# A routed-attention and expert kernel: the first tiles' token numbers move one turn later and into another bank

## The chip, the cores and the metric

The kernel runs on one core of a Trainium2 chip. A time is device microseconds (us) of one execution; before the change the median of three runs was 732.02 us (731.34 to 732.61). The profile is of one further execution, with a span of 725.9 us, and all times inside it count from its start.

The names of the engines: PE is TensorE (matrix products), PEld its weight loads, DVE is VectorE, ACT is ScalarE, POOL is GpSimd, SP is the engine that issues most transfers.

## The reference

Attention, in which a query sees only the keys of its own cluster, and then a layer of eight experts, of which each token goes to one:

```python
# q, k, v: (4, 8, 768, 64); centroids: (8, 16, 64); clusters by cosine similarity
mask = q_assign[:, :, :, None] == k_assign[:, :, None, :]
scores = np.where(mask, q @ k.T / 8, -1e9)                 # per batch and head
x = softmax(scores) @ v                                    # then (B*S, H*D) = (3072, 512)

logits = x @ w_gate                                        # (3072, 8)
expert_idx, gate_w = argmax(logits), softmax(logits)[expert_idx]
y = gate_w * (relu(x @ w1[expert_idx]) @ w2[expert_idx])   # w1: 512 -> 1024, w2: 1024 -> 512
```

## The kernel before

The attention goes through 16 pairs of heads (`g`, four pairs to each of four batches), two **turns** to a pair, so 32 turns. A turn has six scores (blocks of 128 keys against 384 queries for both heads), some jobs, six attends (values times the exponentials), and more jobs. A table, filled by `at(turn, part, function, ...)`, says which job is recorded where; the engines keep that order, each for itself:

```python
for n in range(-4, NTURN + 5):
    for x in range(n * NB, (n + 1) * NB):      # NB = 6
        if 0 <= x < NU:
            score(x)
        if x == n * NB + 2:
            for f, a in jobs.get((n, 2), ()): f(*a)      # part 2: between the scores
    for f, a in jobs.get((n, 0), ()): f(*a)              # part 0: before the attends
    for x in range(n * NB, (n + 1) * NB):
        if 0 <= x < NU:
            attend(x)
    for f, a in jobs.get((n, 1), ()): f(*a)              # part 1: after them
```

A score takes one of three double banks of PSUM, named `sps`; `wide()` hands out the same three to other work. The bank `mps` is a single one, for sums and small things. `T` gathers the exponentials' sums on VectorE:

```python
def score(u):
    ps = ps_s.tile([P, 2, 512], F32, name="sps")          # bufs=3
    # two products q.k (L991), two with the clusters' one-hots ohT (L994)
    nc.scalar.activation(A[u], ps[:, :, 0:HS], AF.Exp, scale=D**-0.5)     # L996
    # T <- A[u-1] + A[u] (L999), then T <- T + A[u] (L1003), on VectorE

def attend(u):      # twelve products O <- v, A in all for a turn (L1011)
def finish(g, half):                                       # after the attends of a half
    nc.scalar.copy(XT[g][...], O.pop((g, half))[...])      # L1019
def similar(g):     # clusters of the pair to come
    ps = wide()[:, 0, :]
    ...
    nc.vector.transpose(sims[g], ps[:, 0:HS])              # L911
def put_k(g):       # their one-hots go to ohT by four transfers on the SP queue (L961)
def weigh(g):       # denominators and gate logits of a pair
    ps = ps_m.tile([P, 512], F32, name="mps")
    ...             # 8 products with T, 4 with xT (L1033)
    nc.vector.transpose(ls, ps[:, 0:SQ])                   # L1041
    # reciprocal on VectorE; three or four small operations on GpSimd (the last pair: VectorE)
def keep(g, c0, c1):      # the pair's rows, undivided, to DRAM: a transpose (L1060), 4 transfers by GpSimd (L1062)
def keep_pads(b):         # the batch's factors for its rows: 16 transfers on the SP queue (L1097)
```

The experts' work begins inside the attention. When three of four batches are through the gate, the tokens of experts 0 and 1 among them fill the "first tiles" (288 and 128 tokens). Their numbers come out of one-hot products; `spread` turns them into row indices; GpSimd gathers the rows, 32 tokens to an issue; VectorE multiplies them by their factors and turns them; then the first layer's products can run:

```python
def tokens1():
    ps = wide()[:, 0, 0 : 2 * NP]
    tokens(ps, oh_r1, oh_c1, NF)                  # 18 products (L688)
    rc1[1] = indices(pl, ps, NP, s_idx1)          # seven small VectorE operations (L695 to L709)
def spread1():                                    # four products into mps (L716), five VectorE operations (to L723)
def gather1(i):                                   # 9 issues for i = 0, 4 for i = 1 (L289)
def turn_rows1(i):
    divide_rows(g)                                # VectorE, L302
    turn_rows(g)                                  # VectorE, L305
def first_half(i, f0=0, f1=FB):                   # layer 1 of first tile i (L318), relu on ScalarE (L328)

n = (NG - HP) * TG                                # turn 24
at(n + 4, 1, tokens1)
at(n + 5, 2, spread1)
for i in range(len(FT)):
    at(n + 5, 2, gather1, i)
at(n + 6, 1, turn_rows1, 0)
at(n + 7, 1, turn_rows1, 1)
```

After turn 31 come the first tile's products, the last pair's weighing, the gate of the last batch, and then the routing of all the rest (counts L642, token numbers, gathers) beside the second layer of the first tile (L383), and the remaining experts.

Of the kernel before, what the change touches and what calls it, by code (L numbers as in the profile page):

```python
# [8 lines left out]
F32 = mybir.dt.float32  # L9
# [11 lines left out]
NB = 6  # L21
XU = 8
RQ = 32
FT = ((128, 128, RQ), (128,))

NP = sum(len(n) for n in FT)
# [159 lines left out]
def kernel(  # L186
# [12 lines left out]
    B, H, S, D = q.shape  # L199
    C = centroids.shape[1]  # L200
    P = 128
# [3 lines left out]
    HP = H // 2  # L205
    NG = B * HP
# [27 lines left out]
    def fetch1(e, i):  # L234
        w1 = wpool.tile([P, DB, F], F32, name=f"w1_{i % 2}")
        nc.sync.dma_start(out=w1, in_=moe_w1[bass.ds(e, 1)].rearrange("e (a p) f -> p (e a) f", p=P))
        return w1

    def fetch2(e, i):
        w2 = wpool.tile([P, FB, Dm], F32, name=f"w2_{i % 2}")  # L240
        nc.sync.dma_start(out=w2, in_=moe_w2[bass.ds(e, 1)].rearrange("e (a p) d -> p (e a) d", p=P))
        return w2
# [25 lines left out]
    ps_m = late.enter_context(tc.tile_pool(name="ps_m", bufs=1, space=PSUM))  # L268
# [9 lines left out]
    def wide():  # L278
        return pools["s"].tile([P, 2, 512], F32, name="sps")
# [406 lines left out]
    def tokens(ps, oh_r, oh_c, n):  # L686
        for t in range(n):
            nc.tensor.matmul(  # L688
                ps, lhsT=oh_r[:, t, :], rhs=oh_c[:, t].rearrange("p i w -> p (i w)"), start=(t == 0), stop=(t == n - 1)
            )  # L690
# [11 lines left out]
    def indices(pool, ps, w, si):  # L702

        parts = pool.tile([P, 2 * w], BF16, name="hlb")
        nc.vector.tensor_copy(parts, ps)
        tv, ta = numbers(pool, ps[:, 0:w], ps[:, w : 2 * w], [P, w])
        nc.vector.tensor_scalar(tv, tv, scalar1=0.0, scalar2=float(2 * N), op0=ALU.is_lt, op1=ALU.mult)
        nc.vector.tensor_add(tv, tv, ta)
        nc.vector.tensor_copy(si, tv)  # L709
        return parts  # L710
# [21 lines left out]
    with ExitStack() as actx:  # L732
# [66 lines left out]
        ps = ps_m.tile([P, 512], F32, name="mps")  # L799
# [184 lines left out]
        def score(u):  # L984
            g, half, j = where(u)
            qs = slice(half * HS, (half + 1) * HS)
            ks = slice(j * P, (j + 1) * P)
            ps = ps_s.tile([P, 2, 512], F32, name="sps")
            for a in range(2):
                r = slice(a * D, (a + 1) * D)  # L990
                nc.tensor.matmul(ps[:, a, 0:HS], lhsT=qk[g][r, 1, ks], rhs=qk[g][r, 0, qs], start=True, stop=False)  # L991
            for a in range(2):
                r = slice(a * D, (a + 1) * D)
                nc.tensor.matmul(ps[:, a, 0:HS], lhsT=ohT[g][r, 1, ks], rhs=ohT[g][r, 0, qs], start=False, stop=True)  # L994
            A[u] = ap.tile([P, 2, HS], F32, name="A")
            nc.scalar.activation(A[u], ps[:, :, 0:HS], AF.Exp, scale=D**-0.5)  # L996
            if j == 1:
                T[g, half] = tp_.tile([P, 2, HS], F32, name="T", bufs=3)
                nc.vector.scalar_tensor_tensor(  # L999
                    T[g, half], in0=A[u - 1], scalar=1e-9 / P, in1=A[u], op0=ALU.add, op1=ALU.add  # L1000
                )
            elif j > 1:
                nc.vector.tensor_tensor(T[g, half], T[g, half], A[u], op=ALU.add)  # L1003

        def attend(u):
            g, half, j = where(u)
            if j == 0:
                O[g, half] = ps_o.tile([P, 512], F32, name="O")
            a_ = A.pop(u)
            for a in range(2):  # L1010
                nc.tensor.matmul(  # L1011
                    O[g, half][a * D : (a + 1) * D, 0:HS], lhsT=rows[g, "v"][:, a, j, :], rhs=a_[:, a, :],
                    start=(j == 0), stop=(j == NQ - 1),
                )
# [90 lines left out]
        def at(n, part, f, *a):  # L1105
            jobs.setdefault((n, part), []).append((f, a))
# [3 lines left out]
        TG = UG // NB  # L1110
# [4 lines left out]
        for g in range(NG):  # L1115
            n = g * TG
            if g == 0:
                at(-4, 0, turn, g, 0)
                at(-4, 0, load_next)
                at(-4, 0, blocks)  # L1120
                at(-4, 1, turn, g, 1)
                at(-3, 0, similar, g)
                at(-3, 0, assign, g)
                at(-3, 0, assign2, g)
                at(-3, 0, put, g)
            elif g == 1:
                at(-2, 1, idle_of, 20)
                at(0, 0, turn_blocks, g)
                for f in (similar, assign, assign2, put_k):
                    at(0, 1, f, g)  # L1130
                at(1, 0, put_q, g)
            else:
                at(n - 3, 0, turn_blocks, g)
                at(n - 2, 0, similar, g)
                at(n - 2, 0, assign, g)
                at(n - 2, 1, assign2, g)
                at(n - 2, 1, put_k, g)
                at(n - 1, 0, put_q, g)
            at(n, 1, finish, g, 0)
            at(n + 1, 1, finish, g, 1)  # L1140
            if g < NG - 1:
                at(n + 2, 0, weigh, g)
                at(n + 2, 1, keep, g, 0, S)
                if g % HP == HP - 1:
                    at(n + 3, 0, gate, g // HP)
                    at(n + 4, 0, gate2, g // HP)
                    at(n + 5, 0, keep_pads, g // HP)


        front = parts[0]  # L1150
# [13 lines left out]
            one_hots(pl, rc1[0], slice(i * NF // 2, (i + 1) * NF // 2), k_["tiles"], oh_r1, oh_c1)  # L1164

        def tokens1():
            ps = wide()[:, 0, 0 : 2 * NP]
            tokens(ps, oh_r1, oh_c1, NF)
            rc1[1] = indices(pl, ps, NP, s_idx1)

# [21 lines left out]
        n = (NG - HP) * TG  # L1192
# [2 lines left out]
        at(n + 2, 1, slots1)  # L1195
        at(n + 3, 0, one_hots1, 0)
        at(n + 3, 1, one_hots1, 1)
        at(n + 4, 1, tokens1)
        at(n + 5, 2, spread1)
        for i in range(len(FT)):  # L1200
            at(n + 5, 2, gather1, i)
        at(n + 6, 1, turn_rows1, 0)
        at(n + 7, 1, turn_rows1, 1)

        n = NG * TG
        at(n - 1, 0, keep, NG - 1, 0, HS)
        at(n, 0, keep, NG - 1, HS, S)
        at(n, 0, first_half, 0, 0, FB // 4)
        at(n, 0, weigh, NG - 1)
        at(n, 0, gate, B - 1)  # L1210
        at(n, 0, gate2, B - 1)
        at(n, 0, keep_pads, B - 1)
        at(n, 1, first_half, 0, FB // 4, FB // 2)
        at(n + 1, 0, first_half, 0, FB // 2, FB)
        for g in range(2, NG):
            at(max(g * TG - 6, -1), 1, load_qk, g)
            at(max(g * TG - 5, -1), 1, load_v, g)

        def early(e, i):

            if i == 0:
                weights[e] = (
                    wpool.tile([P, DB, F], F32, name=f"w1_{e}"), wpool.tile([P, FB, Dm], F32, name=f"w2_{e}"),
                )
            for w, src in zip(weights[e], (moe_w1, moe_w2)):
                n = w.shape[1] // DB
                nc.scalar.dma_start(
                    out=w[:, i * n : (i + 1) * n, :],
                    in_=src[e, i * n * P : (i + 1) * n * P, :].rearrange("(a p) f -> p a f", p=P),
                )  # L1230
# [5 lines left out]
        for n in range(-4, NTURN + 5):  # L1236
            for x in range(n * NB, (n + 1) * NB):
                if 0 <= x < NU:
                    score(x)
                if x == n * NB + 2:  # L1240
                    for f, a in jobs.get((n, 2), ()):
                        f(*a)
            for f, a in jobs.get((n, 0), ()):
                f(*a)
# [3 lines that stand above are left out]
            for f, a in jobs.get((n, 1), ()):  # L1248
                f(*a)
# [7 lines left out]
    with tc.tile_pool(name="sm", bufs=1) as sm:  # L1257
# [20 lines left out]
        for part in parts:  # L1278
            n, over = part["n"], part["over"]
# [97 lines left out]
    g = groups[0]  # L1377
# [58 lines left out]
    with tc.If(more > 0):  # L1436
        nx = nc.values_load(xe[0:1, NX : NX + 1], min_val=0, max_val=NX)
        general = nc.values_load(xe[0:1, NX + 1 : NX + 2], min_val=0, max_val=1)
        with tc.If(nx > XU):
            with ExitStack() as ectx:  # L1440
# [3 lines left out]
                with tc.For_i(XU, nx, 1) as i:  # L1444
# [5 lines left out]
                    g = dict(  # L1450
                        n=[P], rows=N, w=(fetch1(ex, 0), fetch2(ex, 0)), gi=lambda j, i: gi[:, i : i + 1],
                        si=lambda j: gi[:, 4:5], apart=False,
                    )
# [37 lines left out]
```

## Time and profile before

| engine | busy, us | share of the span |
|---|---|---|
| PE | 690.4 | 95% |
| PEld | 443.8 | 61% |
| DVE | 484.8 | 67% |
| ACT | 265.7 | 37% |
| POOL | 249.8 | 34% |

The table is the first part of the page. A share is an average over all stages; a change in one stage has to be read there. The other parts used below are the span in 40 slices (a digit is the busy share in tenths), the chain of work that ended last, followed back from the end, and the timeline: start and length in us, engine, line, operation, output and inputs, shapes and count, and in brackets how long the engine was idle before and what released it. "Remote" there means that no instruction or transfer in the trace ended when the awaited signal came.

Where the stages lie: turns 24 to 31 run from 268.95 to 353.5 us; turn 28's first score starts at 298.44, turn 29's at 309.81, turn 30's at 327.82, turn 31's at 338.00. The first tile's products run from 353.52 to 370.6, the second layer's from 370.82.

### The profile page before, as it was taken

To read this page: it belongs to the slowest core of one execution; us is meant where nothing else is said; L and a number is where in the kernel's file an instruction comes from. 1 tells how busy PE (TensorE), PEld (TensorE's weight loads), DVE (VectorE), ACT (ScalarE), POOL (GpSimd) and SP (SyncE) were. 2 spreads that over 40 slices of the span, in tenths; PEclk is the share of its full clock that TensorE was granted. 3 is DMA by queue.
4 is the path that set the end of the run, shared out by engine and by line. 5 is a ranking of instruction groups with operands and counts; after the bars stand their busy time and mean duration, and the time that the engine had idled before them with its cause. 6 is when DMAs were issued, how large, how long until landed. Compare 5 with 4: busy or idle time off the path is not lost.

```text
span 725.9 us, 12017 instructions
## 1 busy us (share of the span) xinstructions
PE 690.4 (95%) x4603; PEld 443.8 (61%) x4603; DVE 484.8 (67%) x769; ACT 265.7 (37%) x410; POOL 249.8 (34%) x327
## 2 busy tenths in 40 slices
PE   8999999999999999968999888999999999999994
PEld 6444444444444444433566647888878788987861
DVE  5898888878898789984555443967566756645300
ACT  4566556666556555633211012131211212121100
POOL 4022221222222221347305754445446363413101
PEclk9999999999999999989899999999999999999997
DMA  8345677787666644221234143778576667748530
GB/s 149 64 88 92 130 149 148 130 145 139 123 118 114 109 82 85 31 31 47 44 119 163 53 154 115 296 267 287 165 279 210 245 230 273 268 155 306 211 133 19
DMA packets 152420, 108.20 MB, mean 149 GB/s; under 512 B 116513, under 2 KB 122529, under 8 KB 152354
## 3 DMA queue, kind: packets, MB, share of 16 engines
q1 hardware_dynamic: 138146, 78.89, 40.0%
q0 software_dynamic: 8640, 19.63, 11.9%
q10 hardware_dynamic: 5568, 8.83, 4.1%
q8 instruction: 38, 0.62, 0.4%
q14 instruction: 28, 0.23, 0.1%
HBM read 93.06 MB, written 13.30 MB: 147 GB/s over the span
## 4 chain that ended last, share of the span: by engine, by line
PE 61%; issue 15%; POOL 6%; DVE 6%; SPq 4%; another core or an unknown queue 3%; DMA 3%; ACT 1%; ACTq 0%; POOLq 0%; DVEq 0%
PE sps L991 15%; PE O L1011 12%; PE sps L495 8%; PE sps L318 7%; PE sps L383 5%; PE sps L517 5%; PE sps L994 4%; POOL xg L289 3%; POOL out_dram L338 2%; SPq L1097 2%; PE mps L1033 2%; DMA ohT<-kv 1%; PE sps L354 1%; PE sps L904 1%
## 5 line engine op out<-in xcount | busy, mean ns | idle before, releaser
L991 PE MATMUL sps<-qk 64*128 64x384 f32 x768 | 163.8, 504 | 9.7 <-DVE tv L697 4.3
L289 POOL DMA_INDIRECT xg<-x_rows,g_idx x104 | 118.0, 1134 | 130.4 <-DVE xgT L305 80.2
L996 ACT ACTIVATE A<-sps 128x768 f32<-128x768 f32 x192 | 150.8, 813 | 30.8 <-PE sps L994 29.4
L1003 DVE TENSOR_TENSOR T<-T,A 128x768 f32<-128x768 f32 x128 | 122.7, 958 | 16.5 <-ACT A L996 3.0
L1011 PE MATMUL O<-A,v_in 128*64 128x384 f32 x768 | 131.0, 491 | 0.0
L991 PEld LDWEIGHTS sps<-qk 64*128 64x128 f32 x768 | 68.1, 191 | 64.2 <-issue 45.9
L1011 PEld LDWEIGHTS O<-A,v_in 128*64 128x64 f32 x768 | 52.4, 137 | 74.9 <-issue 72.2
L1045 POOL COPY dens<-ls 128x12 f32<-128x12 f32 x16 | 3.1, 195 | 208.6 <-DVE ls L1041 208.6
L994 PE MATMUL sps<-ohT 64*128 64x384 bf16 x384 | 65.6, 328 | 2.4 <-DMA ohT<-kv 2.4
L383 PE MATMUL sps<-w,h_sb 128*128 128x512 f32 x144 | 65.1, 606 | 2.9 <-DVE h_sb L326 2.9
L338 POOL DMA_INDIRECT out_dram<-zo,s_idx x32 | 37.7, 1177 | 71.6 <-ACT zo L334 28.6
L1019 ACT COPY xT<-O 128x384 f32<-128x384 f32 x32 | 15.3, 478 | 108.8 <-PE O L1011 86.7
L318 PEld LDWEIGHTS sps<-xgT,w 128*128 128x128 f32 x448 | 51.0, 192 | 3.7 <-issue 3.7
L1062 POOL DMA_DIRECT2D x_rows<-xb x68 | 48.4, 719 | 10.9 <-DVE xb L1060 8.3
L318 PE MATMUL sps<-xgT,w 128*128 128x128 f32 x448 | 51.3, 275 | 0.0
L999 DVE SCALAR_TENSOR_TENSOR T<-A 128x768 f32<-128x768 f32 x32 | 30.6, 957 | 29.4 <-ACT A L996 29.0
L383 PEld LDWEIGHTS sps<-w,h_sb 128*128 128x128 f32 x144 | 27.3, 194 | 34.9 <-issue 31.1
L495 PE MATMUL sps<-xs,w1s 128*128 128x144 f32 x288 | 39.7, 293 | 3.3 <-issue 3.1
L495 PEld LDWEIGHTS sps<-xs,w1s 128*128 128x128 f32 x288 | 37.1, 193 | 8.9 <-issue 4.7
L994 PEld LDWEIGHTS <-ohT 64*128 64x128 bf16 x384 | 20.5, 95 | 29.2 <-DMA ohT<-kv 4.4
L361 ACT COPY zc<-sps 32x512 f32<-32x512 f32 x24 | 13.9, 578 | 60.5 <-PE sps L354 49.3
L328 ACT ACTIVATE h_sb<-sps 128x512 f32<-128x512 f32 (+1 forms) x18 | 9.6, 578 | 69.5 <-PE sps L318 59.9
(260 smaller groups left out, 922.2 us busy)
## 6 DMA issues: line engine op xcount, KB each, us to landing
w<-in_moe_w_dram SPq DMA_DIRECT2D x28, 2048.0 KB, 9.3
w<-in_moe_w_dram ACTq DMA_DIRECT2D x16, 512.0 KB, 6.2
v_in<-in_v_dram SPq DMA_DIRECT2D x16, 384.0 KB, 4.4
q_in<-in_q_dram SPq DMA_DIRECT2D x60, 96.0 KB, 3.6
k_in<-in_k_dram SPq DMA_DIRECT2D x60, 96.0 KB, 6.3
x_rows<-xb POOLq DMA_DIRECT2D x60, 96.0 KB
xg<-x_rows,g_idx POOLq DMA_INDIRECT x104
ohT<-kv SPq DMA_DIRECT2D x60, 24.0 KB, 4.6
```

The costliest lines, as they stand in the source:

```text
L289: nc.gpsimd.indirect_dma_start(out=g["xg"][:, n, :], out_offset=None, in_=x_q[0 : 4 * g["rows"], :], in_offset=bass.IndirectOffsetOnAxis(a ...
L318: nc.tensor.matmul(o, lhsT=g["w"][0][:, c, fb * P : (fb + 1) * P], rhs=g["xT"][:, c, :cols], start=(c == 0), stop=(c == DB - 1),)
L338: ins = nc.gpsimd.indirect_dma_start(out=out[:, :], out_offset=bass.IndirectOffsetOnAxis(ap=g["si"](j)[0:m], axis=0), in_=zo[0:m], in_offs ...
L383: nc.tensor.matmul(zp, lhsT=g["h"][:, fb, j * P : (j + 1) * P], rhs=g["w"][1][:, fb, :], start=(fb == 0), stop=(fb == FB - 1),)
L495: nc.tensor.matmul(o, lhsT=a[:, c, f * P : (f + 1) * P], rhs=b[:, c, :], start=(c == 0), stop=(c == KH - 1),)
L517: nc.tensor.matmul(ps[:, 0, 0:DH], lhsT=a[:, f, :], rhs=b[:, f, :], start=(f == 0), stop=(f == FH - 1),)
L991: nc.tensor.matmul(ps[:, a, 0:HS], lhsT=qk[g][r, 1, ks], rhs=qk[g][r, 0, qs], start=True, stop=False)
L994: nc.tensor.matmul(ps[:, a, 0:HS], lhsT=ohT[g][r, 1, ks], rhs=ohT[g][r, 0, qs], start=False, stop=True)
L996: nc.scalar.activation(A[u], ps[:, :, 0:HS], AF.Exp, scale=D**-0.5)
L1003: nc.vector.tensor_tensor(T[g, half], T[g, half], A[u], op=ALU.add)
L1011: nc.tensor.matmul(O[g, half][a * D : (a + 1) * D, 0:HS], lhsT=rows[g, "v"][:, a, j, :], rhs=a_[:, a, :], start=(j == 0), stop=(j == NQ - 1),)
L1062: nc.gpsimd.dma_start(out=x_d[b * S + c0 : b * S + c1, quad, hp * 32 : (hp + 1) * 32].rearrange("(n t) d -> t n d", t=32), in_=xb[quad * 3 ...
```

## The change

The three parts, in the author's words: rows' factors queued behind clusters and loads; first tiles' token numbers found a turn later in the sums' bank; last pair's sums ahead of the first tile.

1. `keep_pads` of the first three batches is recorded after the jobs of the turn before, behind that turn's `put_k` and `load_qk`, so that its sixteen transfers don't stand in front of theirs.
2. `tokens1` moves from the end of turn 28 to between the fifth and sixth score of turn 29, and from a bank of `sps` to `mps`; `spread1` and the nine gathers of the first tile move behind the attends of turn 29, the four of the second tile behind those of turn 30; the first tile's turning moves behind the scores of turn 31 and the second's behind the gate of the last batch. It is meant to take the token sums out of the banks that the scores use.
3. In the turn after the last, `weigh` of the last pair and its rows are recorded ahead of the first tile's products.

```diff
-                    at(n + 5, 0, keep_pads, g // HP)
...
         def tokens1():
-            ps = wide()[:, 0, 0 : 2 * NP]
+            ps = ps_m.tile([P, 512], F32, name="mps")[:, 0 : 2 * NP]
...
-        at(n + 4, 1, tokens1)
-        at(n + 5, 2, spread1)
-        for i in range(len(FT)):
-            at(n + 5, 2, gather1, i)
-        at(n + 6, 1, turn_rows1, 0)
-        at(n + 7, 1, turn_rows1, 1)
+        at(n + 5, 2, tokens1)
+        at(n + 5, 1, spread1)
+        at(n + 5, 1, gather1, 0)
+        at(n + 6, 1, gather1, 1)
+        at(n + 7, 0, turn_rows1, 0)
 
         n = NG * TG
         at(n - 1, 0, keep, NG - 1, 0, HS)
+        at(n, 0, weigh, NG - 1)
         at(n, 0, keep, NG - 1, HS, S)
         at(n, 0, first_half, 0, 0, FB // 4)
-        at(n, 0, weigh, NG - 1)
         at(n, 0, gate, B - 1)
         at(n, 0, gate2, B - 1)
         at(n, 0, keep_pads, B - 1)
+        at(n, 0, turn_rows1, 1)
...
+        for b in range(B - 1):
+
+            at((b + 1) * HP * TG + 2, 1, keep_pads, b)
...
-                if x == n * NB + 2:
+                if x == n * NB + 4:
                     for f, a in jobs.get((n, 2), ()):
```

## The prediction

> **What bounds the kernel now.** I read the page first: TensorE is busy 95% of the span, so only stretches in which it is not can give anything. In the 40 slices of 18.1 us the first dip below 9 after the start is at the 18th and 19th slice (308 to 345 us), and the chain that ended last has an entry, "another core or an unknown queue", of which 9.2 us lie there.
>
> ```profile
> PE   8999999999999999968999888999999999999994
> PE 61%; issue 15%; POOL 6%; DVE 6%; SPq 4%; another core or an unknown queue 3%; DMA 3%; ACT 1%; ACTq 0%; POOLq 0%; DVEq 0%
> ```
>
> Next the timeline of that stretch, engine by engine. The kernel works in turns: six scores, then six attends, then jobs. TensorE (start, length, line, tiles; in brackets the idle time and who ended it):
>
> ```profile
> 298.44 0.92 PE L991 MATMUL sps<-qk 64*128 64x384 f32 x4
> ...
> 309.27 0.61 PE L688 MATMUL sps<-oh_c,oh_r 128*128 128x8 bf16 x18
> 309.81 0.92 PE L991 MATMUL sps<-qk 64*128 64x384 f32 x4
> ...
> 312.61 0.92 PE L991 MATMUL sps<-qk 64*128 64x384 f32 x4 [1.73 <-DVE sim L911]
> ...
> 317.97 1.65 PE L991 MATMUL sps<-qk 64*128 64x384 f32 x4 [4.28 <-DVE tv L697]
> ...
> 323.80 4.09 PE L1011 MATMUL O<-A,v_in 128*64 128x384 f32 x24
> 327.82 0.92 PE L991 MATMUL sps<-qk 64*128 64x384 f32 x4
> ...
> 333.98 4.09 PE L1011 MATMUL O<-A,v_in 128*64 128x384 f32 x24
> ...
> 344.29 1.65 PE L991 MATMUL sps<-qk 64*128 64x384 f32 x4 [3.60 <-ACT A L996]
> ...
> 349.40 4.19 PE L1011 MATMUL O<-A,v_in 128*64 128x384 f32 x24
> ```
>
> An undisturbed turn's scores take 5.05 us (298.44 to 303.49). Turn 29's take 14.0 (309.81 to 323.80): of its first three scores the second finds its bank of `sps` held by `similar`, the third by the token sums, until VectorE has read them. Turn 31's take 11.4 (338.00 to 349.40), for another reason, to be seen on ScalarE, VectorE and GpSimd:
>
> ```profile
> 317.48 0.17 DVE L705 CAST hlb<-sps 128x8 bf16<-128x8 f32 x1
> 318.63 0.95 DVE L999 SCALAR_TENSOR_TENSOR T<-A 128x768 f32<-128x768 f32 x1
> 338.38 1.36 DVE L302 TENSOR_TENSOR xg<-xg 128x1152 f32<-128x1152 f32 x1 [0.25 <-DMA xg<-x_rows,g_idx]
> 323.11 1.71 POOL L289 DMA_INDIRECT xg<-x_rows,g_idx  x1 [5.32 <-DVE g_idx L723]
> 335.85 0.94 POOL L289 DMA_INDIRECT xg<-x_rows,g_idx  x1 [0.30 <-issue]
> 340.87 0.94 POOL L289 DMA_INDIRECT xg<-x_rows,g_idx  x1 [0.30 <-issue]
> 343.05 0.48 ACT L1019 COPY xT<-O 128x384 f32<-128x384 f32 x1 [9.26 <-remote]
> ```
>
> ScalarE's copy of O waits for TensorE alone in the program. TensorE's attends end at 338.07, the copy starts at 343.05: the signal is 5 us late. The thirteenth gather in a row has just been issued (340.87 to 341.81). The same is seen once more: the layer-1 products of 406.60 to 417.04 release VectorE and ScalarE both at 422.99, 2.2 us after another run of gathers. Early in a run it doesn't happen: attends that end at 327.82 release the copy at 327.94, in a run begun at 323.11; after 334.05 (11 us into it) the next signal is 2.5 us late. I take it that **TensorE's signals come late toward the end of a long run of gathers**, from some 10 us on, and are free about 1.2 us after its end.
>
> **What the Trainium skill says.** "TensorE: Matmul & The Clock Gate", section "What's actually happening", says that an idle window of about 3.4 us halves the clock until the engine has been busy as long. The trace agrees: the scores after the idle 4.28 and 3.60 us take 1.65 for the 0.81 of before, and the granted clock is 0.76 over 309.3 to 323.8. "Perfetto Trace Analysis", section "Summary: the profiler window per engine type", says that a matmul's end is estimated and the signal's way is hidden; so lateness is read from the waiting engine's start, as above. "DMA: Bandwidth & Descriptors", section "Anatomy of one DMA — SWDGE (gpsimd) path", has about 2 us fixed for a GpSimd transfer; here the ninth gather is issued at 335.85 and its reader starts at 338.38, 2.5 us. No page that I found bears on the late signals.
>
> **The change part by part.**
>
> *Rows' factors.* Compared in the built programs, the sync queue's instructions and waits stand in the same order before and after: clusters (L961), q and k loads, sixteen writes of factors (L1097), then the v load. Nothing lay on this queue between the old place and the new one. **0 us.** The delay that the chain shows at 222 to 234 us (factors, then `ohT`) therefore stays.
>
> *Token numbers a turn later, in `mps`.* Until the attends of turn 28 end (309.3) nothing changes. Turn 29 then has no tokens in front, so the third score, not the second, meets `similar`'s bank, free at 312.6. The third to sixth scores take 0.92 + 3 x 0.81, the tokens 0.6: 316.5; attends 4.1: **320.6**. VectorE is the engine that matters next: it finishes the clusters at 317.45 as now and goes straight on with the sums of turn 29: 0.95 + 3 x 1.04 = 4.1, to 321.6; seven small operations on the tokens (317.48 to 318.72 now: 1.24), to 322.8; the last sum, 323.9; the five of `spread` (321.76 to 322.82 now: 1.06), to 325.0. TensorE's `spread` needs the tokens' bank read by the third of the small operations, 322.1, so it waits 1.5 us and turn 30 starts at **322.5** instead of 327.82: **5.3 us won**. The `ohT` of that turn, issued at 317.2 to 320.3 and last moved at 322, is then just in time.
>
> *Gathers.* They start at 325.3, 2.2 later than now, since the sums of turn 29 go ahead. The nine of the first tiles took 13.7 us (323.11 to 336.79, with VectorE's sums beside them): to 339.0; the last is issued at 338.1 and its rows can be read 2.5 later, **340.6**. The four of the second expert follow apart, after the rows of pair 14 (four operations and four issues, 1.3 + 2.9 us): 343.5 to 348.5, with nothing near that needs them, for their turning now stands after the gate.
>
> *Turn 30, turn 31.* Turn 30 with its weighing took 10.2 us (327.82 to 338.00): 332.7. Turn 31's scores would end at 337.8 and its sums at 339.5. But a run of gathers from 325.3 reaches its tenth us at 335.3, so I expect the signals of the last three scores (ends 335.3, 336.1, 336.9) to come at about 340.2. Their exponentials, 0.81 each, end at 342.7; attends at 344.3; the sums at 344.0. VectorE then multiplies and turns the first tile, 1.36 + 1.38 = 2.75: **346.8**.
>
> *Last pair's weighing ahead of the first tile.* It needs the sums (344.0) and xT (344.8) and takes 1.1: about 346, beside that multiplying. So it fills a gap, and the 32 products (64 records) of the first tile start at 346.8 and run 4.1 + 11.9 = 16.0 us without a break: **362.8**. Now:
>
> ```profile
> 358.71 11.91 PE L318 MATMUL sps<-xu,w 128*128 128x288 f32 x48
> 370.45 0.28 PE L642 MATMUL mps<-pr_b,lt_strict 128*128 128x8 f32 x2
> ```
>
> The end comes 7.6 us earlier. On VectorE the weighing, the gate, the second tile's turning (0.65 + 0.71) and the last batch's choice then take from 346 to about 354, hidden behind the products as they are now (done 363.3 against 370.45). What follows hangs on this point: the count L642, the weight load issued at 370.65, the token numbers and the gathers of the rest. I see no other clock in it, so it all moves by the same 7.6. 732.0 - 7.5 = **724.5 us**.
>
> **Rivals.**
> 1. *Signals in time.* With nine gathers in place of thirteen the run may be too short for lateness. Then the gathered rows set the pace: 340.6 + 2.75 = 343.4, products to 359.4, 11 us won: 721. For it: signals up to 332.95 are punctual, ten us into the present run. Against it: the runs from 402 and from 426 us show signals some us late after six to ten.
> 2. *Signals late from further forward.* If that of turn 30's attends (332.7) is already held until 340.2, the whole of turn 31's exponentials follow it: 340.7 to 345.6, sums 346.8, first tile 349.6, products to 365.6; 4.8 us won, 3 if the clock drops too: 727 to 729. For it: the late signal in the run from 426 us comes after some seven us. The three cases are one question: which signal is the first to be held.
> 3. *VectorE or GpSimd becomes the bound.* VectorE has no gap from 306 to 325, and moving the index arithmetic behind four sums delays the gathers by 2.2 us. If sums beside gathers slow them more (four of the nine took 1.5 to 1.7 us instead of 0.95), each adds 0.7 to the 340.6. Two more: 1.5 us less gain.
> 4. *Hidden anyway.* The win is in front of a routing stage with waits of its own; if a weight load were last there, part would be given back. But the load of 370.65 is released by the products themselves and L383 after them takes 14 us of TensorE, so I give this little.
>
> **Range and chances.** The cases give wins of 11, 7.6 and 3 to 5; the runs before lie within 1.3 us. Range: 719.5 to 729.5. Faster by over 2% would need 14.6 us, more than the stalls of turns 29 and 31 leave after the rows' own path: 0.03. Slower by over 2% would need a wait that I don't see: 0.01.
>
> **What would show it.** Turn 29: tokens to `mps` between its fifth and sixth score, one wait on `sim`, none on `tv` before the scores, turn 30's first score near 322.5. If that is off, the VectorE sum is wrong. Gathers: the first near 325.3, nine in a row. Turn 31: idle before its exponentials at 335 to 340 "<-remote" is my middle case; none at all rival 1; before the copy of O rival 2. First tile's products in one row from about 347. L1097 in the same places as now. The prediction fails if the run of gathers holds a signal longer than 8 us, or if later runs of gathers, shifted against the weight loads, hold theirs for another length.

## The result, and the profile after

The changed kernel takes 722.86 us (median of 4 runs, 718.66 to 723.55) for 732.2 before (4 runs beside it): 9.3 us less. The ratio is 0.987, 95% interval 0.983 to 0.990, so the gain is clear of noise and below 2%. A fifth run on record took 724.11. 724.5 had been predicted, with 719.5 to 729.5 as the range. Both profiled executions lie below their medians, by 4.2 and 4.5 us (after 718.66, before 727.65), so the two traces differ by nearly the measured gain, 9.0.

From the page of the kernel after, TensorE's row of slices, the granted clock's, and the chain's shares by engine:

```profile
PE   8999999999999899989998779999999999999994
PEclk9999999999999999999999999999999999999998
PE 52%; issue 16%; DVE 12%; POOL 7%; SPq 4%; DMA 3%; another core or an unknown queue 3%; ACT 1%; ACTq 0%; DVEq 0%; POOLq 0%
```

The 18th slice was 6 and is 8, the 19th was 8 and is 9. The dip that is left lies at the 22nd to 24th slice (376 to 430 us, slices of 17.9), in the experts' stage; it was there before as well, at the 23rd to 25th. The chain's shares tell little of the change: VectorE's has grown from 6% to 12%, by 45 us, but only 8 of these lie at 309 to 345 us, and most lie ahead of 309 us, where the change hardly touches the work. The timeline of TensorE after, from turn 29 to the end of the first tile's products (start, length, line, tiles, in brackets the idle time and who ended it):

```profile
309.88 0.92 PE L991 MATMUL sps<-qk 64*128 64x384 f32 x4
...
313.22 0.92 PE L991 MATMUL sps<-qk 64*128 64x384 f32 x4 [1.46 <-DVE sim L911]
...
315.85 0.61 PE L688 MATMUL mps<-oh_c,oh_r 128*128 128x8 bf16 x18
...
322.64 0.24 PE L716 MATMUL mps<-hlb,to_quarters 128*128 128x8 bf16 x4 [1.16 <-DVE tv L697]
322.81 0.92 PE L991 MATMUL sps<-qk 64*128 64x384 f32 x4
...
338.04 4.09 PE L1011 MATMUL O<-A,v_in 128*64 128x384 f32 x24
342.06 0.86 PE L1033 MATMUL mps<-T,one_row 128*32 128x192 f32 x16
...
344.13 15.76 PE L318 MATMUL sps<-xu,w 128*128 128x288 f32 x64 [0.89 <-DVE xu L305]
359.73 0.28 PE L642 MATMUL mps<-pr_b,lt_strict 128*128 128x8 f32 x2
```

Turn 29 has one wait in front of a score where it had two, and its scores take 7.5 us (309.88 to 317.39) for 14.0. Turn 31's take 5.05 (332.99 to 338.04) for 11.4. The first tile's 64 records stand in one row. ScalarE after, where before the copy of O had waited 9.26 us, and below it VectorE's last sums of turn 31, and its multiplying and turning of the first tile's rows:

```profile
333.11 0.48 ACT L1019 COPY xT<-O 128x384 f32<-128x384 f32 x1 [4.33 <-issue]
...
338.34 1.57 ACT L996 ACTIVATE A<-sps 128x768 f32<-128x768 f32 x2 [1.00 <-PE sps L994]
```

```profile
339.19 2.02 DVE L1003 TENSOR_TENSOR T<-T,A 128x768 f32<-128x768 f32 x2 [0.34 <-ACT A L996]
341.12 1.45 DVE L302 TENSOR_TENSOR xg<-xg 128x1152 f32<-128x1152 f32 x1
342.61 1.38 DVE L305 STREAM_TRANSPOSE xu<-xg 128x1152 f32<-128x1152 f32 x1
```

The copy follows the attends (end 333.06) at once, and only the last two exponentials wait, for 1 us. VectorE takes up the rows directly behind the last sum.

### The profile page after: what moved, and what is told of

It reads as the page before. It is cut to its first block, busy times and chain, and to the rows that moved or that the text cites. A ratio compares the mean times of both kernels' runs of the same rounds, so it can differ in the third digit from the quotient of the medians.

```text
span 716.9 us, 12015 instructions
## 1 busy us (share of the span) xinstructions
PE 686.9 (96%) x4603; PEld 443.2 (62%) x4603; DVE 484.6 (68%) x769; ACT 266.9 (37%) x410; POOL 251.1 (35%) x327
## 3 DMA queue, kind: packets, MB, share of 16 engines
q0 software_dynamic: 8640, 19.63, 12.4%
## 4 chain that ended last, share of the span: by engine, by line
PE 52%; issue 16%; DVE 12%; POOL 7%; SPq 4%; DMA 3%; another core or an unknown queue 3%; ACT 1%; ACTq 0%; DVEq 0%; POOLq 0%
PE sps L991 11%; PE O L1011 9%; PE sps L495 8%; PE sps L318 6%; PE sps L383 6%; PE sps L517 5%; DVE T L1003 4%; POOL xg L289 3%; PE sps L994 3%; DMA ohT<-kv 2%; POOL out_dram L338 2%; SPq L1097 2%; PE sps L354 1%; PE mps L1033 1%
## 5 line engine op out<-in xcount | busy, mean ns | idle before, releaser
L991 PE MATMUL sps<-qk 64*128 64x384 f32 x768 | 159.6, 493 | 1.6 <-DVE sim L911 1.5
L495 PE MATMUL sps<-xs,w1s 128*128 128x144 f32 x288 | 41.3, 297 | 3.1 <-issue 3.0
L361 ACT COPY zc<-sps 32x512 f32<-32x512 f32 x24 | 13.9, 579 | 60.8 <-PE sps L354 49.6
```

Of the source, the lines that this page charges most:

```text
L495: nc.tensor.matmul(o, lhsT=a[:, c, f * P : (f + 1) * P], rhs=b[:, c, :], start=(c == 0), stop=(c == KH - 1),)
```

## One table for all traces

The lengths below are read from each kernel's profiled execution on TensorE's timeline, from the end of turn 28's attends to the first count after the first tile (L642; L648 or L650 where lines are added). It is cut at the attends of turns 29, 30 and 31: "T29" is from the end of turn 28's attends to the start of turn 29's, and so on; an undisturbed turn has 5.0 there, 6.1 with a weighing. "All" is the four columns and the three turns' attends, 4.1 us each. The runs came in five sets, A to E, B to E on four different chips; on which chip A ran is not on record. In three sets (A, B, D: the kernel before takes 732, 742 and 736 us by the median) signals of TensorE come late in runs of gathers; in two (C and E: 710 and 715) the traces show no late signal in any run of gathers, so there they are "prompt". The kernel before has a trace in set A alone. Ratios to the kernel before are within a set, with 95% intervals; they can differ from the ratio of the medians by some 0.2%.

| kernel | set | T29 | T30 | T31 | to count | all | ratio |
|---|---|---|---|---|---|---|---|
| before | A, late | 14.5 | 6.1 | 11.3 | 16.9 | 61.1 | 1 |
| after | A, late | 7.5 | 7.5 | 5.0 | 17.6 | 49.8 | 0.987 (0.983-0.990) |
| g13_row | B, late | 7.1 | 8.1 | 13.6 | 16.7 | 57.8 | 0.996 (0.993-0.998) |
| split_only | B, late | 14.2 | 8.7 | 5.0 | 16.9 | 57.0 | 0.990 (0.987-0.993) |
| weigh_after | B, late | 7.0 | 7.8 | 9.3 | 17.4 | 54.0 | 0.991 (0.988-0.994) |
| bank_only | B, late | 10.9 | 6.1 | 12.4 | 16.9 | 58.5 | 0.996 (0.994-0.998) |
| after_here | C, prompt | 7.5 | 7.5 | 5.0 | 17.7 | 49.9 | 0.993 (0.990-0.995) |
| late_sps | C, prompt | 7.5 | 7.2 | 5.0 | 17.7 | 49.6 | 0.990 (0.986-0.993) |
| break_13 | C, prompt | 14.5 | 6.1 | 5.0 | 16.9 | 54.7 | 1.000 (0.998-1.002) |
| rows_first | C, prompt | 7.4 | 7.5 | 5.0 | 17.8 | 50.0 | 0.996 (0.994-0.998) |
| break_again | D, late | 14.6 | 8.4 | 5.0 | 16.9 | 57.1 | 0.995 (0.993-0.997) |
| split_again | D, late | 15.2 | 6.1 | 5.0 | 16.9 | 55.4 | 0.995 (0.993-0.997) |
| after_third | E, prompt | 7.1 | 7.5 | 5.0 | 18.1 | 50.0 | 0.991 (0.989-0.994) |
| rests | E, prompt | 7.5 | 7.7 | 5.0 | 18.1 | 50.5 | 0.990 (0.987-0.993) |

Two theories stood at the start. **Mine**: part of the gain is the earlier turn 30, the rest comes from signals of TensorE that are late in an unbroken row of gathers, which the change cuts in two. **Rival**: the second part comes from something else that the split changes, the number of gathers near the scores or the order of GpSimd's sums and stores.

## Experiments: the row of gathers

**g13_row**: the changed kernel, with the second tile's gathers put back behind the first's.

```
-        at(n + 6, 1, gather1, 1)
+        at(n + 5, 1, gather1, 1)
```

> The changed kernel with the thirteen gathers in one row again, as before the change (the four of the second tile directly behind the nine). Late signals: if TensorE's signals are held toward the end of a long run of gathers, the run from 325.5 us now lasts to about 342.5, the signals of turn 31's last scores come only near 343.7 instead of 338.3 to 339.1, and with them its exponentials and sums: 3 to 5 us are lost, 726 to 728 us. Rival, the length of the run doesn't matter and turn 31 was slow before for another reason: within 1 us of the changed kernel, about 723.

Measured: 739.35 us for 742.32 before. Most of the gain is gone. ScalarE's timeline in turn 31:

```profile
347.64 0.48 ACT L1019 COPY xT<-O 128x384 f32<-128x384 f32 x1 [7.81 <-PE sps L994]
...
352.68 0.81 ACT L996 ACTIVATE A<-sps 128x768 f32<-128x768 f32 x1 [2.74 <-PE sps L994]
354.91 2.21 ACT L996 ACTIVATE A<-sps 128x768 f32<-128x768 f32 x3 [1.42 <-remote]
```

The attends had ended at 344.12, so the copy's signal is 3.5 us late, and the two exponentials shown start 6.8 and 8.2 us after their scores had ended (345.93 and 346.74). The gathers run from 335.93 to 352.9 in a row. The loss against the changed kernel of set A, 8.0 us in the table, is larger than the 3 to 5 that I had expected.

**split_only**: the reverse, the kernel before with only the four gathers moved.

```
-        for i in range(len(FT)):
-            at(n + 5, 2, gather1, i)
+        at(n + 5, 2, gather1, 0)
+        at(n + 6, 1, gather1, 1)
```

> The kernel before, with the four gathers of the second tile moved behind the attends of turn 30 and nothing else. Late signals: the run of nine ends at 336.8, the signal of turn 30's attends comes in time or 1 to 2 us late instead of 5, turn 31's scores take 5 to 7 us instead of 11.4: 5 us won, about 727. The token sums stay in the scores' banks, so turn 29 still takes 14. Rival, the run's length doesn't matter: as before, 732.

Measured: 736.02 us, 6.3 less than before (742.32). Turn 29 is as bad as ever (its longer wait, on TensorE's timeline), but turn 31 is whole (on ScalarE's):

```profile
330.12 1.65 PE L991 MATMUL sps<-qk 64*128 64x384 f32 x4 [4.27 <-DVE tv L697]
```

```profile
348.76 1.51 ACT L996 ACTIVATE A<-sps 128x768 f32<-128x768 f32 x2 [2.03 <-remote]
353.12 0.48 ACT L1019 COPY xT<-O 128x384 f32<-128x384 f32 x1 [2.84 <-PE O L1011]
354.12 4.85 ACT L996 ACTIVATE A<-sps 128x768 f32<-128x768 f32 x6 [0.52 <-PE sps L994]
```

The signals of turn 30 were late here (up to 348.76), those of turn 31 not. Both theories allow this; the next experiment tells them apart.

**break_13**: the kernel before, with all thirteen gathers where they were, and a pause of GpSimd among them.

```
+    def rest(k):
+        for _ in range(k):
+            nc.gpsimd.memset(idle_t, 0.0)
...
             gather(g)
+            if i == 0:
+                rest(3)
```

> The kernel before, with three fills of a scratch tile on GpSimd (about 1.35 us each, 4 us in all) between the ninth and the tenth of the thirteen gathers that stand in one row; they are neither split over two turns nor fewer, and the second tile's four come 4 us later. Theory that TensorE's completion signals are held while GpSimd issues one gather behind another without a pause: the signals of turn 31's scores come through in the pause, the stall of turn 31 (scores over 8 us or more instead of 5) shrinks to 2 us or less, and the time falls by 4 to 7 us, as in the kernel before with the gathers split (ratio 0.990). Rival, that the number of gathers near the scores or the traffic of their rows does it: thirteen gathers and 4 us of further GpSimd work leave the stall as it was, and the time is that of the kernel before or up to 4 us more.

Measured: 710.31 us for 709.86, no gain. But on chip C signals are prompt. ScalarE in this trace:

```profile
340.32 0.48 ACT L1025 COPY xT<-O 128x384 f32<-128x384 f32 x1 [4.33 <-PE O L1017]
341.32 4.85 ACT L1002 ACTIVATE A<-sps 128x768 f32<-128x768 f32 x6 [0.52 <-PE sps L1000]
```

The copy comes at once after the attends (end 340.27), and the six exponentials in one piece. Nor is a signal late in the experts' stage, where gathers run in rows of nine and more without the pause. So there was nothing to win, and I ran it again, with the split beside it.

**break_again** and **split_again**: the same two kernels.

> The pause between the ninth and the tenth of thirteen gathers once more, since in the last four runs, on a chip whose kernel before took 710 us, no signal of TensorE was held anywhere (their traces show none), so that there was nothing for the pause to win (ratio 1.000). If this chip holds signals, as the chips with 732 and 742 us did: the theory of the unbroken row says that the pause lets the signals of turn 31's scores through, ratio 0.990 to 0.994, as the split did there; the rival, the number of gathers, says 1.000 to 1.005. If this chip holds none: 1.000 again, and the theory isn't tested.

> The kernel before with the second tile's four gathers moved a turn later, as in the run on the 742 us chip, where it won 7.4 us (ratio 0.990). If its gain came through held signals alone, it follows the chip: 0.988 to 0.993 where signals are held, and nothing (0.998 to 1.003) where they are not. Rival: the split wins by GpSimd's sums and stores coming ahead of the four gathers, which would win on every chip, 0.990 on this one too whichever it is.

Measured on chip D, where signals are late: 730.99 and 731.29 us for 735.59, ratios 0.995 (0.993 to 0.997) both. GpSimd and ScalarE of the kernel with the pause:

```profile
339.51 0.94 POOL L295 DMA_INDIRECT xg<-x_rows,g_idx  x1 [0.30 <-issue]
340.45 4.27 POOL L262 MEMSET idle_t<- 128x1536 bf16 x3
344.87 0.95 POOL L295 DMA_INDIRECT xg<-x_rows,g_idx  x1 [0.16 <-issue]
```

```profile
341.88 1.51 ACT L1002 ACTIVATE A<-sps 128x768 f32<-128x768 f32 x2 [2.03 <-PE mps L1039]
346.03 0.48 ACT L1025 COPY xT<-O 128x384 f32<-128x384 f32 x1 [2.63 <-PE O L1017]
347.04 3.23 ACT L1002 ACTIVATE A<-sps 128x768 f32<-128x768 f32 x4 [0.53 <-PE sps L1000]
```

Exponentials of turn 30 wait for signals until 341.88, 1.4 us after the ninth gather's end and the start of the pause (340.45); from then on nothing is late by more than 0.3 us, the copy comes at once after the attends (end 345.99), although four more gathers are being issued. Thirteen gathers with 4.3 us of added GpSimd work in their midst gain what the split gains: the number of gathers is not the cause, and neither is the order of GpSimd's sums. **The unbroken row is.** What in the row holds the signals, the issuing or the transfers that it starts, is not told apart: the ninth gather's own transfer runs until 341.8, just before the signals come (DMA moves 97 GB/s at 341.10 to 341.80 and nothing from then to 344.8). The gain of both, 0.5%, is less than the 0.6 to 1.0% and the 0.7 to 1.2% that I had put down for the pause and the split, and less than the split's 1.0% on chip B: what the late signals cost differs from chip to chip.

## Experiments: the token numbers, and the weighing

**bank_only**: the kernel before with the token sums in `mps`, at their old place.

```
-            ps = wide()[:, 0, 0 : 2 * NP]
+            ps = ps_m.tile([P, 512], F32, name="mps")[:, 0 : 2 * NP]
```

> The kernel before, with the token sums in the bank of mps but at their old place, the end of turn 28. Theory: mps is one bank and holds turn 28's weighing until VectorE has read it at 311.9 us, so TensorE stands still before the tokens from 309.3 to about 312 with all scores behind it; the third score's wait of 4.3 us goes, but spread after it waits for VectorE at 317.9, so the scores of turn 29 end at about 321 instead of 323.8: 2 to 3 us won at most, 729 to 730. Rival, the bank alone was the matter: turn 29 as quick as in the changed kernel, 5 us won, 727.

Measured: 740.57 us, a ratio of 0.996 to 742.32 before: 1.8 us less by the medians, 2.8 by the ratio; two to three had been expected. The waits on TensorE have moved to the head of the turn:

```profile
324.06 0.61 PE L688 MATMUL mps<-oh_c,oh_r 128*128 128x8 bf16 x18 [2.07 <-DVE ls L1041]
...
330.11 0.24 PE L716 MATMUL mps<-hlb,to_quarters 128*128 128x8 bf16 x4 [1.13 <-DVE tv L697]
```

The sums now wait for the weighing's result, which lies in the same bank. T29 takes 10.9 us, for 14.2 in split_only of the same set, where the token sums stand as before the change. Turn 31 is late here too (12.4).

**late_sps**: the changed kernel, tokens a turn later, but in a bank of the scores.

```
-            ps = ps_m.tile([P, 512], F32, name="mps")[:, 0 : 2 * NP]
+            ps = wide()[:, 0, 0 : 2 * NP]
```

> The changed kernel with the first tiles' token numbers found a turn later, but still in a bank of the scores, as before the change. If the turn later carries this part, the time is that of the changed kernel (within 0.3%): the scores of turn 30 start at 322.8 in its trace, after the numbers' bank has been read (322.4), so a third score bank is not missed. If the bank in which they lie carries it, the fourth tile of scores waits for the bank, turn 30 starts up to 3 us later, and the time is 2 to 3 us above the changed kernel's.

**after_here**: the changed kernel itself, beside it and beside break_13 and rows_first.

> The changed kernel itself, run beside the three below so that they have it on their own chip. Both theories: the ratio to the kernel before that the result had, 0.987 (0.983 to 0.990). If it stands above 0.991 here, the attention stage of this chip, where runs of the kernel before showed more waiting for transfers, hides a part of the gain, and the single parts are to be held against the value found here.

Measured: 704.08 us, and 705.82 for the changed kernel. The intervals overlap; it isn't slower. TensorE of late_sps:

```profile
324.53 0.24 PE L716 MATMUL mps<-hlb,to_quarters 128*128 128x8 bf16 x4 [0.88 <-DVE hlb L705]
```

The wait ahead of turn 30 is 0.88 us for 1.15 in after_here. Together with bank_only: at the old place the bank is worth 3.3 us of T29, a turn later it is worth nothing, as VectorE has read the numbers before the next scores ask for any bank. It is the turn later that carries this part.

**weigh_after**: the changed kernel with the last pair's weighing behind the first quarter of the products again.

```
-        at(n, 0, weigh, NG - 1)
...
         at(n, 0, first_half, 0, 0, FB // 4)
+        at(n, 0, weigh, NG - 1)
```

> The changed kernel with the last pair's weighing behind the first quarter of the first tile's products again. If it fills a gap of TensorE (342.1 to 344.1 us in the changed kernel's trace), putting it behind the products adds its 1.1 us to the path: about 724. Rival, the path is elsewhere: no change, 722.9. Too small for the times alone; the trace's stage from turn 31's last attend to the count L642 decides (17.7 us in the changed kernel, 18.8 expected).

Measured: 735.57 us for 742.32 before, 0.991. It stands 0.4% behind the ratio of the changed kernel on chip A, but turn 31 had late signals in its trace (9.3), so the difference can't be put down to the weighing. From the end of the attends to the count it has 17.4 us, the changed kernel 17.6 to 18.1; the 18.8 that I had expected did not come. With the rows turned late here (the products wait 0.47 us for them), the weighing's place is not resolved: no run shows a gain from it.

## Experiments: more of it in the experts' stage

**rows_first**: the changed kernel with the third tile's rows turned ahead of the weights' sums.

```
-    for f in sums_w1(groups[1]):
-        f()
     g = groups[0]
...
     turn_of(g)
+    for f in sums_w1(groups[1]):
+        f()
```

> The changed kernel with one thing more: in the stage of the experts, the division and the turning of the third tile's rows (0.82 and 0.84 us) stand ahead of the four sums of the weights (4.9 us) on VectorE, since in the changed kernel's trace TensorE is idle for 3.13 us ahead of that tile's products (395.98) and waits for the turned rows, whose VectorE work stood behind those sums (389.49 to 394.14). If nothing else held these products, they start 3 us earlier and the kernel ends 3 us earlier (ratio to before lower by 0.004). Rival: the rows, gathered from 385 on, come late or the next hold-up (the signals held at 403.8 and 412.5 in the row of gathers) takes it all back: no gain, as the end of that row of gathers, not TensorE's start, then sets the next stage.

Measured: 707.22 us for 709.86 before, and 705.82 for the changed kernel beside it; the rival held. On chip C TensorE idles 1.81 us ahead of that tile in the changed kernel. Here, on its timeline, that wait is gone, and another of its size has come:

```profile
396.35 8.86 PE L318 MATMUL sps<-xu,w 128*128 128x160 f32 x64
...
415.88 2.20 PE L495 MATMUL sps<-xs,w1s 128*128 128x144 f32 x16 [1.95 <-DVE xs L405]
```

VectorE's `xs` waits for the next nine gathers, and these stand behind a store of rows that VectorE's sums release at 391.9.

**rests**: the same, with those nine gathers ahead of that store, and pauses in the later rows of gathers.

```
+                if n == 5 and g.get("pause"):
+                    rest(2)
...
-    adds[0]()
     gather_of(groups[1])
+    adds[0]()
...
+    rest(2)
     gather_of(groups[2])
```

> The changed kernel with what the runs point to in the experts' stage: two fills (2.7 us) on GpSimd after the fifth of each run of nine gathers and ahead of the third group's four, so that no more than nine gathers stand in one row; the second group's nine gathers put ahead of the rows' store that held them up (392.18 in the trace with the rows turned first); and the third tile's rows turned ahead of the weights' sums, whose 1.8 us that trace shows won at TensorE and lost again to the late gathers. If held signals cost the changed kernel 2.96 us at 413.06 and some 2.5 us at 428 to 430, as its trace on the 732 us chip shows, and the 1.8 us stay won: 4 to 7 us faster than the changed kernel where signals are held, 1.5 to 2 us where none are. Rival: the experts' stage is bound by something that these stalls hide (the products of the next weights, the stores at the end), and the time is that of the changed kernel, within 1 us.

**after_third**: the changed kernel beside it.

> The changed kernel once more, beside the kernel below. Theory of two parts: 0.7% (5 us) come from the earlier turn 30 and are there on every chip; a further 0.4 to 0.6% come where TensorE's signals are held in the kernel before. So the ratio is 0.985 to 0.990 if this chip holds signals, 0.991 to 0.995 if it holds none.

Measured in set E, without late signals: 708.45 us, and 709.03 for the changed kernel, with ratios of 0.990 (0.987 to 0.993) and 0.991 (0.989 to 0.994): the same within their spread. TensorE of rests:

```profile
369.54 0.28 PE L650 MATMUL mps<-pr_b,lt_strict 128*128 128x8 f32 x2
...
419.50 2.23 PE L503 MATMUL sps<-xs,w1s 128*128 128x144 f32 x16
```

Neither wait of 1.8 us is there, and from the count to the sums' first product it takes 50.0 us (369.54 to 419.50) for 52.0 in the changed kernel's trace (366.17 to 418.17); but the times don't show the 2 us: 1.5 to 2 us had been expected on such a chip, and the rival held. The first row has ten gathers (389.05 to 402.35), one more than the expectation says. What the pauses are worth where signals are late, which is what they were made for, wasn't measured.

## Why the prediction was right, step by step

- **Rows' factors, 0 us.** No run took this part alone. The traces agree with it: the three runs of sixteen writes (L1097) start at 142.20, 222.46 and 296.49 us, for 141.76, 222.16 and 295.98 before.
- **Token numbers, 5.3 us.** Right. From the end of turn 28's attends to turn 30's first score it is 12.9 us (309.94 to 322.81) for 18.5 before (309.34 to 327.82), 5.6 won. The turn starts at 322.81 for a predicted 322.5, in a trace that runs 0.6 late from turn 28 on. The wait before `spread`, given as 1.5, was 1.16. Where signals are prompt this step is all that is left to win, and the changed kernel is 4.0 and 5.5 us faster by the medians (ratios 0.993 and 0.991).
- **The gathers.** First at 325.52 (325.3 predicted), the ninth issued 336.93 to 338.60 (end 339.0 predicted). Rival 3's further slowing did not come: three of the nine took over 1.5 us, of the nine before four took 1.47 to 1.74.
- **Which signal is held first.** Here the middle case failed in size. It held the last three scores' signals to 340.2; only the last two exponentials waited, until 338.34, for 1 us, and the tile was turned at 343.99, where rival 1 had 343.4 and the middle case 346.8. That is close to rival 1's time, but not by its path: rival 1 let the gathered rows set the pace, and in the trace VectorE takes up the rows without a wait, behind the sums of turn 31, the last of which waited for these exponentials. So the tile is turned 2.8 us sooner than I had summed, and the stretch from turn 28 to the count gained 11.3 us for my 7.6. Nor is it a fixed tenth us of a run from which signals are held: weigh_after, in set B, has nine gathers in a row as here, and took 9.3 us for turn 31.
- **"It all moves by the same."** Wrong by 1.7 us. From the count to the end it is 357.2 us (716.9 - 359.73) for 355.4 (725.9 - 370.45). The prediction had named a danger here, that later runs of gathers hold their signals for another length; the longest such stall does not bear it out. ScalarE and TensorE there, after and then before:

```profile
412.52 0.44 ACT L328 ACTIVATE h_sb<-sps 128x320 f32<-128x320 f32 x1 [8.25 <-remote]
413.06 5.35 PE L383 MATMUL sps<-w,h_sb 128*128 128x512 f32 x8 [2.96 <-DVE h_sb L326]
...
422.99 0.44 ACT L328 ACTIVATE h_sb<-sps 128x320 f32<-128x320 f32 x1 [9.56 <-remote]
423.54 5.40 PE L383 MATMUL sps<-w,h_sb 128*128 128x512 f32 x8 [2.90 <-DVE h_sb L326]
```

After, TensorE's products for the first line had ended at 406.56, 6.0 us before it; before the change such a signal was 5.8 us late (417.21 to 422.99), and TensorE idled as long. From the count to the first L517 it is 87.25 us for 87.05. The rest of the 1.7 lies later: the five iterations from there take 42.5, 42.1, 42.1, 42.1 and 41.9 us for 41.9 to 42.0 before (1.15 us together), and the end 0.4. In the first of them TensorE waits 0.33 us; what lengthens the others is open. 11.3 less 1.7 is 9.6, near the traces' 9.0 with the 0.6 us that the profiled execution lost ahead of turn 28.

- **Last pair's weighing fills a gap.** It does (342.06 to 343.24, before 344.13), and 0.89 us of the gap is left: the turned rows are the limit there.

So the whole came out within 1.6 us, and that is in part luck: a stretch that gained 3.7 us more than summed met a later one that gave 1.7 back. That an unbroken row of gathers makes signals of TensorE late is now shown, and its worth can be estimated: the stretch of the kernel before takes 61.1 us in set A, and 54.7 where signals are prompt (the paused kernel, whose pause had nothing to win there). That is 6.4 us of late signals, of which the split took 6.3 in turn 31, and 4.9 of the earlier turn 30 less the gap that is left (54.7 to 49.8), seen in every set in which the changed kernel ran (A, C, E).

**Open** are the cause of the lateness itself, the issuing of gathers or their transfers, and why two of the chips don't have it. The kernel before has no trace on a prompt chip of its own; the paused kernel, equal to it in time there (1.000), stands for it.

## What to carry to other kernels

Read a wait "<-remote" or one on an engine that had long been done together with what GpSimd issues at that time: a long row of its gathers can hold back TensorE's signals. Cut the row by work that has to be done anyway (here sums and stores of another pair): that won 0.5 to 1.0% where signals were late, and where they were prompt even a pause of 4.3 us that did nothing else cost nothing (1.000). A result that an engine has to read out of a score bank is best put at the end of a turn, with the reader's other work in front of the next demand; then the bank in which it lies no longer matters. When a wait is taken away in front of a stage, look at the next wait of the same size before counting it as won (rows_first: 1.81 us off, 1.95 on).

## What the runs showed of the hardware

- Chips differ in it: the same kernel before took 710 to 742 us, and in the changed kernel the stretch from the count to the first product of the second layer's sums (L517) takes 73.0 us in set C (363.74 to 436.71) and 87.3 in A (359.73 to 446.98). In A TensorE idles 10.3 us of it for 2.4 in C, and its granted clock is 0.94 for 1.00. That the 14 us are late signals is likely, as A's trace has them there and C's has none, but no run took them away.
- The signals themselves come late, not only the reader's start: the trace before has TensorE's semaphore updates for the ends at 338.07, 339.08, 339.88 and 340.69 at 343.03, 343.10, 343.18 and 343.25, one close behind the other.
- Signals are let through 1.4 us after a pause begins on GpSimd (340.45 to 341.88), with fills running on it: that GpSimd is busy does not hold them.
- The clock drops behind long waits, but the length of one wait doesn't decide it. "TensorE: Matmul & The Clock Gate", section "What's actually happening", in the Trainium skill puts the halving at an idle window of about 3.4 us. In turn 29 after, whose longest wait is 1.46, the granted clock is 1.00 (0.76 before) and no score takes 1.65 us; in bank_only the score behind 3.87 us of idleness does. But shorter waits are enough in some traces: the score behind 1.74 us in break_13 (314.74) takes 1.65 us and the first behind 2.07 us in bank_only (324.60) takes 1.58, while the score behind 1.73 us before (312.61) and the one behind 3.25 us in g13_row (349.99) take 0.92.
